# A state-space layer and a gated feed-forward block on one core: who copies the first turned quarter of tile 1, where tile 2 is turned, and the order of the fourth contraction step

## The chip, the cores and the metric

The kernel runs on one core of one Trainium2 chip. The metric is the time of one execution on the device in microseconds (us); the median of several runs is compared. Names used below: TensorE (PE) multiplies matrices and loads their stationary operands as separate instructions (PEld); VectorE (DVE), ScalarE (ACT) and GpSimd (POOL) work on elements; SyncE (SP) issues most DMAs. SBUF is the on-chip memory that all engines read; PSUM is the memory that TensorE writes, here eight banks of 128 partitions by 512 fp32 numbers.

## The reference

For `x` of 2048 tokens by 512 channels in bf16:

```
xn = layernorm(x)                                   # over the 512 channels
A  = state space: Bu = xn @ B_bar^T (complex, 512 states)
     h[t] = Lam_bar * h[t-1] + Bu[t];  2 * Re(h @ C^T) + xn * Dskip
B  = (gelu(xn @ w_gate) * (xn @ w_up)) @ w_down     # w_gate, w_up: 512 x 1376, w_down: 1376 x 512
out = x + A + B
```

The parts that this document is about are the first two products of B, `xn @ w_gate` and `xn @ w_up`, for the first 512 tokens.

## The kernel before

The tokens are worked in four blocks of 512, each block in four tiles of 128 tokens. For most of the kernel TensorE goes through `GU` (gate and up products, L843), `BU` (the input of the states, L749) and `DN` (the product with `w_down` and the states' output, L884), while VectorE runs the recurrence (L787).

The first block has to start before anything is normalised, while the weights are still arriving, and that start is what is changed here. Its tiles are not normalised first: a tile is only centred (the mean is subtracted, L961 for tiles 0 and 1, L950 for tiles 2 and 3), turned on TensorE (`cent_T`, L684, four transposes of 128 columns into one PSUM bank), and copied from PSUM into `XC` by ScalarE (L689). The division by the standard deviation comes later, as a scale of the gelu. The turned tile is the stationary operand of the gate and up products of its 128 tokens, so that the results have tokens on the partitions. The contraction over 512 channels has four steps `k`, each of which needs one quarter of the turned tile and one chunk of 128 rows of each weight; the chunks come as DMAs of 128 KB, gate and up in turn (L488).

For tiles 0, 1 and 2 and the first 512 of the 1376 columns the accumulation is spread out, one step at a time, so that a step can run as soon as its chunk has landed: `GT_k(k, j, u, ws)` (L701) is one matmul of step `k`, tile `j` and column half `u`, with `ws` telling whether it takes the gate weights (`[0]`, 256 columns), the up weights (`[1]`, 256 columns) or both side by side (`[0, 1]`, 512 columns). `ks(k, j, ws)` issues it for both halves. Six PSUM banks (`acc(j, u)`) hold the six running sums, gate in one half of the bank and up in the other; banks 6 and 7 take the transposes. After the fourth step `GT_evac` lets ScalarE take the gelu (L721) and VectorE multiply (L724). The ten groups that remain (tile 3, and columns 512 to 896 of all four tiles) run with all four steps at once in `GT_mm` (L712), tile 3 first:

```
        for (j, u), bank in zip([(3, 0), (3, 1), (0, 2), (0, 3), (1, 2), (1, 3), (2, 2), (2, 3), (3, 2), (3, 3)],
                                (6, 7, 0, 1, 2, 3, 4, 5, 0, 7)):
            GT_mm(j, u, bank)
            GT_evac(j, u, bank)
```

So the first `GT_mm` needs the whole of tile 3 in `XC`.

Order. TensorE and SyncE run their instructions in the order in which the source issues them. For VectorE, ScalarE and GpSimd a planner (`Sched`) sorts the instructions by costs written into the source; operations that are passed through `ch` stay in the order in which they were chained. A wait is a semaphore that the instruction itself, or a separate instruction just in front of it, waits for. An engine stands still at such a wait, and all that is queued behind it stands still too; only weight loads of TensorE are seen to run ahead of the matmul before them.

In front of the first groups TensorE runs seven matmuls on constants (L933). VectorE takes statistics with `stats` (L615, L616) and centres tile 2 after the statistics of tiles 0 and 2; those of tiles 1 and 3, the centring of tile 3, and the norms (L634) whose DMA transposes (`TR`, L736, on SyncE) feed the later `GU` of the same block come behind.

Of the kernel before, what the change touches and what calls it, by code (L numbers as in the profile page):

```python
# [9 lines left out]
ALU = mybir.AluOpType  # L10
# [336 lines left out]
L, D, P, F = 2048, 512, 512, 1376  # L347
# [7 lines left out]
def d_pe(n_list):  # L355
    return sum(n / 2.4 + 2.5 for n in n_list)
def d_dve_tt2x(n): return 100.0 + 0.52 * n
def d_dve_1x(n): return 100.0 + 1.04 * n
def d_dve_scan(n): return 90.0 + 2.08 * n
def d_dve_ts4x(n): return 220.0 + 0.26 * n  # L360
D_TINY = 160.0
def d_act(n, ptr=0): return 190.0 + 0.833 * n + 90.0 * ptr
# [3 lines left out]
def build(nc, ins, out):  # L366
    with ExitStack() as es:
# [6 lines left out]
        BANK = [Buf("bank%d" % i, "ps", i, i + 1) for i in range(8)]  # L374

        def ring(parent, name, n):
            return [A.sub(parent, "%s%d" % (name, i), i) for i in range(n)]
# [14 lines left out]
        X = ring(X_all, "X", NT)  # L392
        XN_all = A.alloc("XN", [8, D], BF16)
        XN = ring(XN_all, "XN", 8)
        DSKB = A.alloc("DSKB", [D], BF16)
        XD_all = A.alloc("XD", [NT, D], BF16); XD = ring(XD_all, "XD", NT)
        IDN = A.alloc("IDN", [128], BF16)
# [8 lines left out]
        MVt = [[A.sub(MV[b], "MV%d_%d" % (b, j), j) for j in range(4)] for b in range(NB)]  # L406
# [58 lines left out]
        V = lambda fn, dur, r, w, tag="", after=(): S.op("vector", fn, dur, r, w, tag, after)  # L465
        ACT = lambda fn, dur, r, w, tag="", after=(): S.op("scalar", fn, dur, r, w, tag, after)
        POOL = lambda fn, dur, r, w, tag="", after=(): S.op("gpsimd", fn, dur, r, w, tag, after)
        PE = lambda fn, dur, r, w, tag="": S.op("tensor", fn, dur, r, w, tag)
# [39 lines left out]
        def load_par():  # L508
            for q, nm in enumerate(("A_log_dt", "A_Lambda_re", "A_Lambda_im")):
                GATE["par"] = S.order_behind(S.dma(lambda e, q=q, nm=nm: e.dma_start(PROW.ap[4 * q:4 * q + 4, :], ins[nm].rearrange("(s p) -> s p", p=128)),  # L510
                      1024, writes=[PROWq[q]], tag="ld_" + nm, queue="scalar", after=[half]), GATE["par"])
            GATE["par"] = S.order_behind(ld_x0(2, "scalar"), GATE["par"])
# [100 lines left out]
        def stats(b, j):  # L613
            tt = 4 * b + j
            return (V(lambda e: e.bn_stats(ST[tt].ap, X[tt].ap), d_dve_1x(512), [X[tt]], [ST[tt]], "bnst"),  # L615
                    V(lambda e: e.bn_aggr(MVt[b][j].ap, ST[tt].ap), D_TINY, [ST[tt]], [MVt[b][j]], "bnag"))  # L616

        def root(b, j0, j1):
            mn, sbq, qb, rq = (cols(t, b, j0, j1) for t in (MN, SBQ, QB, RQ))
            mv = Buf("MV%d_%d_%d" % (b, j0, j1), "sb", MVt[b][j0].lo, MVt[b][j1 - 1].hi, MV[b].ap[:, j0:j1])  # L620
            op = V(lambda e: e.tensor_scalar(sbq.ap, mv.ap[:, :, 1], EPS_BF16, None, ALU.add), D_TINY, [mv], [sbq], "sbq")
            GATE["pow"] = POOL(lambda e: e.tensor_tensor(qb.ap, sbq.ap, HALF.ap[:, 0:j1 - j0], ALU.pow), 1100, [sbq, HALF], [qb], "pow")
            POOL(lambda e: e.tensor_copy(mn.ap, mv.ap[:, :, 0]), 200, [mv], [mn], "mn")
            return op, mn, qb, rq
# [48 lines left out]

        XCd = lambda j, k: XC_all.ap[:, k, 128 * j:128 * (j + 1)]

        XNp = [[Buf("XN%d_%d" % (j, n), "sb", XN[j].lo + 256 * n, XN[j].lo + (1024 if n else 256)) for n in range(2)] for j in range(2)]

        def cent_T(j, k0, k1, bank):
            pt = PS[bank].bitcast(BF16)[:, 0:128 * (k1 - k0)]

            def f(e):
                ins_ = None
                for k in range(k0, k1):
                    ins_ = e.transpose(pt[:, 128 * (k - k0):128 * (k - k0 + 1)], XN[j].ap[:, 128 * k:128 * (k + 1)], IDN.ap)  # L684
                return ins_
            PE(f, 56.0 * (k1 - k0), [XNp[j][k0 > 0] if j < 2 else XN[j], IDN], [BANK[bank]], "T0")
            dst, src = XC_all.ap[:, k0:k1, 128 * j:128 * (j + 1)], pt.rearrange("p (q t) -> p q t", t=128)
            w = XCs[j] if k1 - k0 == KD else [XCs[j][k0 > 0]]
            GATE["evTA"] = ACT(lambda e: e.activation(dst, src, ACTF.Copy), d_act(128 * (k1 - k0)), [BANK[bank]], w, "evT")  # L689

        FR = ((0, 256), (256, 512), (512, 768), (768, 896))

        def acc(j, u):
            return 2 * j + u

        def GT_k(k, j, u, ws, first=False):
            f0, f1 = FR[u]
            w = f1 - f0
            bank = acc(j, u)
            dst = PS[bank][:, w * ws[0]:w * (ws[-1] + 1)].rearrange("p (w f) -> p w f", w=len(ws))  # L700
            PE(lambda e: e.matmul(dst, XCd(j, k), WGU[:, ws[0]:ws[-1] + 1, k, f0:f1], start=first, stop=k == KD - 1, skip_group_check=True),  # L701
               d_pe([w * len(ws)]), [(WGc, WUc)[w_][k] for w_ in ws] + [XCs[j][k > 0]] + ([] if first else [BANK[bank]]), [BANK[bank]], "GK")
# [13 lines left out]
        def GT_evac(j, u, bank):  # L716
            f0, f1 = FR[u]
            w = f1 - f0
            GATE["nh"] = kk = (GATE["nh"] + 1) % 3
            sc, rb = rss[j]  # L720
            GATE["last_gelu"] = ACT(lambda e: e.activation(GG[kk].ap[:, 0:w], PS[bank][:, 0:w], ACTF.Gelu_apprx_tanh, scale=sc),  # L721
                                    d_act(w, 1), [BANK[bank], rb], [GG[kk]], "gelu")
            hp = Buf("H0_%d_%d" % (j, u), "sb", H0[j].lo + 2 * f0, H0[j].lo + 2 * f1)
            V(lambda e: e.scalar_tensor_tensor(H0[j].ap[:, f0:f1], PS[bank][:, w:2 * w], sc, GG[kk].ap[:, 0:w], ALU.mult, ALU.mult),  # L724
              d_dve_1x(w), [BANK[bank], GG[kk], rb], [hp], "hmul")
# [220 lines left out]
        def ch(*ops):  # L946
            for op in ops:
                tail_op[0] = S.order_behind(op, tail_op[0])
        def sub(j):
            return V(lambda e: e.tensor_scalar(XN[j].ap, X[j].ap, MVt[0][j].ap[:, 0:1], None, ALU.subtract),  # L950
                     d_dve_ts4x(512), [X[j], MVt[0][j]], [XN[j]], "sub")
        load_par()
        load_W()
        tr_par()
# [3 lines left out]
        def cent(j, n):  # L958
# [7 lines left out]
                                              op0=ALU.add, op1=ALU.add, accum_out=NM0.ap), 400, [X[0]], [H0[2], NM0], "mean0"))  # L966
        ch(cent(0, 0), cent(0, 1))
        cent_T(0, 0, 1, 7)
        ch(cent(1, 0), cent(1, 1))
        fill(1)  # L970
        cent_T(0, 1, 4, 5)
        def ks(k, j, w_, first=False):
            for u in range(2):
                GT_k(k, j, u, w_, first)
        cent_T(1, 0, 1, 6)
        ks(0, 0, [0], True)
        cent_T(1, 1, 4, 7)
        ks(0, 0, [1])
        ks(0, 1, [0], True)
# [2 lines left out]
        for w_ in range(2):  # L982
            for j in range(2):
                ks(1, j, [w_])
        ks(2, 0, [0]); ks(2, 1, [0]); ks(2, 0, [1])
        ch(*stats(0, 2)); ch(sub(2))
        cent_T(2, 0, 1, 6)
        cent_T(2, 1, 4, 7)
        ks(2, 1, [1])
        ks(0, 2, [0, 1], True)  # L990
        ch(*stats(0, 1))
        op, mn0, qb0, rq0 = root(0, 0, 3)
        ch(op)
        ch(*stats(0, 3)); ch(sub(3))
        ch(recip(qb0, rq0))
        op, mn3, qb3, rq3 = root(0, 3, 4)
# [5 lines left out]
        TR(0, [0, 1])  # L1002
        ks(1, 2, [0, 1])
        ks(2, 2, [0, 1])
        for j in range(3):
            GT_k(3, j, 0, [0, 1])
            if j == 0:
                cent_T(3, 0, 4, 6)
            GT_k(3, j, 1, [0, 1])
            for u in range(2):  # L1010
                GT_evac(j, u, acc(j, u))
        for (j, u), bank in zip([(3, 0), (3, 1), (0, 2), (0, 3), (1, 2), (1, 3), (2, 2), (2, 3), (3, 2), (3, 3)],
# [45 lines left out]
def bass_parallel_sum__ssm_conv_s5__geglu_ffn__prompt_kernel(  # L1058
    nc: bass.Bass,
    A_x: bass.AP,  # L1060
    A_Lambda_re: bass.AP,
    A_Lambda_im: bass.AP,
    A_B_re: bass.AP,
    A_B_im: bass.AP,
    A_C_re: bass.AP,
    A_C_im: bass.AP,
    A_log_dt: bass.AP,
    A_Dskip: bass.AP,
    B_x: bass.AP,
    B_w_gate: bass.AP,  # L1070
    B_w_up: bass.AP,
    B_w_down: bass.AP,
    out: bass.AP,
):
    ins = {
        "A_x": A_x, "A_Lambda_re": A_Lambda_re, "A_Lambda_im": A_Lambda_im,
        "A_B_re": A_B_re, "A_B_im": A_B_im, "A_C_re": A_C_re, "A_C_im": A_C_im,
        "A_log_dt": A_log_dt, "A_Dskip": A_Dskip,
        "B_w_gate": B_w_gate, "B_w_up": B_w_up, "B_w_down": B_w_down,
    }  # L1080
    build(nc, ins, out)
# [28 lines left out]
```

## Time and profile before

| | |
|---|---|
| median of 3 runs | 176.65 us (176.62 to 176.85) |
| profiled execution, its own time | 176.71 us |
| span in the profile, first to last instruction | 175.4 us |
| busy in the span: PE, DVE, ACT, POOL | 98%, 90%, 54%, 6% |
| granted TensorE clock | 1.00 |
| matmuls | 895, of which L701 36, L684 17 |
| first matmul on data; first `GT_mm`; last matmul (start) | 3.71, 10.79, 173.32 us |

A row of the timeline gives the start in us, the length in us (of several instructions in a row, from the first start to the last end), the engine, the line, the operation, what it writes and reads with sizes, how many, and in brackets the idle time of the engine in front of it and what ended that. The chain of waits gives start, length and what the chain that ended last consisted of. A table by stage gives the busy time of each engine in a stretch, with the number of instructions. A group of instructions by line and shape ends with its busy time in us, the mean ns of one, and the idle time in front of it. Matmuls are pipelined: the length of a row is longer than the distance from one start to the next, and it is the distance that costs time. Lines are those of the kernel before.

### The profile page before, as it was taken

Reading aid. Unit: us, or ns where it says so; the run is one execution under the profiler, and the core shown is the slowest. Engines: PE = TensorE matmul, PEld = TensorE weight load, DVE = VectorE, ACT = ScalarE, POOL = GpSimd, SP = SyncE. Lnnn points to the kernel's source line nnn. Section 1 sums busy time; section 2 is a strip of 40 time slices with the busy share of each in tenths; the row PEclk is TensorE's granted clock in tenths of the full one; section 3 lists DMA queues with packets and bytes.
Section 4 is the critical chain, followed back from the end, with each engine's and each line's share of the span. In section 5 each row is a group of like instructions: output and inputs, shape, how many; then the busy total and the mean of one; then the engine's idle time right before and its main releaser. Section 6 shows DMA issues by size and latency. Waiting matters only on the chain.

```text
span 175.4 us, 2533 instructions
## 1 busy us (share of the span) xinstructions
PE 172.7 (98%) x895; PEld 85.0 (48%) x895; DVE 158.5 (90%) x279; ACT 95.2 (54%) x187; POOL 9.9 (6%) x24
## 2 busy tenths in 40 slices
PE   8999999999999999999999999999999999999995
PEld 2646464845544444444644444444464444444454
DVE  5897999987989999789899999997999999999931
ACT  5476678999766997473676792000667970000000
POOL 4122220220000000002000000000000000000000
DMA  5999999477699400002024000002001000000312
GB/s 142 265 340 191 221 206 154 32 130 142 106 250 344 74 0 2 0 30 89 4 53 98 0 0 0 4 0 90 30 0 34 0 0 0 0 0 0 123 62 62
DMA packets 32421, 14.37 MB, mean 82 GB/s; under 512 B 23736, under 2 KB 32408, under 8 KB 32408
## 3 DMA queue, kind: packets, MB, share of 16 engines
q1 hardware_dynamic: 31952, 13.84, 34.6%
q10 hardware_dynamic: 456, 0.36, 0.6%
q8 instruction: 7, 0.11, 0.3%
q14 instruction: 6, 0.05, 0.1%
HBM read 6.46 MB, written 2.10 MB: 49 GB/s over the span
## 4 chain that ended last, share of the span: by engine, by line
PE 98%; DVE 0%; issue 0%
PE PS L884 37%; PE PS L843 32%; PE PS L749 16%; PE PS L712 4%; PE PS L701 3%; PE PS L817 3%; PE PS L933 2%; PE PS L684 1%; DVE arena L902 0%; PE PS L940 0%
## 5 line engine op out<-in xcount | busy, mean ns | idle before, releaser
L884 PE MATMUL PS<-arena 128*128 128x512 bf16 (+3 forms) x323 | 66.2, 366 | 0.0
L843 PE MATMUL PS<-arena 128*128 128x512 bf16 x264 | 58.1, 379 | 0.0
L884 PEld LDWEIGHTS PS<-arena 128*128 128x128 bf16 (+1 forms) x323 | 30.8, 98 | 35.2
L843 PEld LDWEIGHTS PS<-arena 128*128 128x128 bf16 x264 | 25.7, 98 | 30.3
L787 DVE TENSOR_TENSOR_SCAN arena<-arena 128x512 bf16<-128x512 f32 x32 | 38.8, 1252 | 0.0
L858 ACT ACTIVATE arena<-PS 128x512 bf16<-128x512 f32 x33 | 19.7, 598 | 27.0 <-PE PS L843 24.8
L749 PE MATMUL PS<-arena 128*128 128x512 bf16 (+1 forms) x144 | 28.2, 355 | 0.0
L862 ACT ACTIVATE arena<-PS 128x512 bf16<-128x512 f32 x33 | 19.7, 598 | 5.9 <-PE PS L843 5.8
L749 PEld LDWEIGHTS PS<-arena 128*128 128x128 bf16 x144 | 14.1, 98 | 13.3
L876 ACT ACTIVATE PS<-arena 128x512 f32<-128x512 bf16 (+2 forms) x17 | 9.4, 574 | 18.5 <-DVE arena L902 18.0
L758 ACT ACTIVATE arena<-PS 128x512 bf16<-128x512 f32 x32 | 17.4, 596 | 1.5 <-PE PS L749 1.5
L902 DVE TENSOR_TENSOR arena<-PS,arena 128x512 bf16<-128x512 f32 (+2 forms) x17 | 10.9, 652 | 7.8 <-PE PS L884 7.7
L864 DVE TENSOR_TENSOR arena<-arena 128x512 bf16<-128x512 bf16 x33 | 13.2, 413 | 1.8 <-ACT arena L862 1.6
L776 DVE TENSOR_TENSOR arena<-arena 128x4096 bf16<-128x4096 bf16 (+1 forms) x5 | 9.2, 1858 | 0.8 <-ACT arena L611 0.8
L774 DVE TENSOR_TENSOR arena<-arena 128x4096 bf16<-128x4096 bf16 (+1 forms) x5 | 9.2, 1853 | 0.0
L799 DVE TENSOR_TENSOR arena<-arena 128x4096 bf16<-128x4096 bf16 x4 | 9.1, 2286 | 0.0
L800 DVE TENSOR_TENSOR arena<-arena 128x4096 bf16<-128x4096 bf16 x4 | 9.1, 2284 | 0.0
L615 DVE BATCH_NORM_STATS2 arena<-arena 128x6 f32<-128x512 bf16 x12 | 7.8, 681 | 0.4 <-DMA arena<-in_A_x_dram 0.4
L721 ACT ACTIVATE arena<-PS,arena 128x256 bf16<-128x256 f32 (+1 forms) x16 | 6.3, 447 | 1.9 <-DVE arena L724 1.9
L712 PE MATMUL PS<-arena 128*128 128x512 bf16 (+1 forms) x40 | 7.1, 336 | 0.0
L724 DVE SCALAR_TENSOR_TENSOR arena<-PS,arena 128x256 bf16<-128x256 f32 (+1 forms) x16 | 6.2, 442 | 0.3 <-PE PS L701 0.3
L701 PE MATMUL PS<-arena 128*128 128x256 bf16 (+1 forms) x36 | 6.3, 309 | 0.0
(95 smaller groups left out, 123.4 us busy)
## 6 DMA issues: line engine op xcount, KB each, us to landing
out_dram<-arena SPq DMA_DIRECT2D x15, 128.0 KB, 1.7
arena<-in_A_x_dram SPq DMA_DIRECT2D x3, 512.0 KB, 5.3
arena<-in_B_w_down_dram SPq DMA_DIRECT2D x1, 1280.0 KB, 7.3
arena<-in_B_w_gate_dram SPq DMA_DIRECT2D x4, 128.0 KB, 3.3
arena<-in_B_w_up_dram SPq DMA_DIRECT2D x4, 128.0 KB, 3.2
arena<-in_B_w_gate_dram SPq DMA_DIRECT2D x1, 480.0 KB, 6.5
arena<-in_B_w_up_dram SPq DMA_DIRECT2D x1, 480.0 KB, 7.4
arena<-arena SPq DMA_TRANSPOSE x25, 3.1
```

Of the source, the lines that this page charges most:

```text
L701: PE(lambda e: e.matmul(dst, XCd(j, k), WGU[:, ws[0]:ws[-1] + 1, k, f0:f1], start=first, stop=k == KD - 1, skip_group_check=True), d_pe([w ...
L712: ins_ = e.matmul(dst, XCd(j, k), WGU[:, :, k, f0:f1], start=(k == 0), stop=(k == KD - 1))
L749: ins_ = e.matmul(PS[bank][:, 128 * j0:128 * j1], BBT[c][dk].ap[:, 128 * s:128 * (s + 1)], XNT[b].ap[:, dk, 128 * j0:128 * j1], start=(dk ...
L758: GATE["evBu"] = ACT(lambda e, bank=bank, k3=k3, s=s, c=c: e.activation(SSc[k3][s][c].ap, PS[bank][:, :], ACTF.Copy), d_act(512), [BANK[ba ...
L787: V(lambda e, g=g, rb=rb, init=init: e.tensor_tensor_scan(g.ap, rb, g.ap, init, ALU.mult, ALU.add), d_dve_scan(512), [g, PA[RRr]] + ([CARc ...
L843: ins_ = e.matmul(PS[bank][0:m, c0:c1], W.ap[:, dk, 128 * ft:128 * ft + m], XNT[b].ap[:, dk, c0:c1], start=(dk == 0), stop=(dk == KD - 1))
L858: GATE["last_gelu"] = ACT(lambda e, bg=bg, kk=kk, m=m: e.activation(GG[kk].ap[0:m, :], PS[bg][0:m, :], ACTF.Gelu_apprx_tanh), d_act(512), ...
L862: ACT(lambda e, bu=bu, kk=kk, m=m: e.activation(UPB[kk].ap[0:m, :], PS[bu][0:m, :], ACTF.Copy), d_act(512), [BANK[bu]], [UPB[kk]], "evU")
L864: V(lambda e, kk=kk, m=m, ft=ft, k2=k2: e.tensor_tensor(HTt[k2][ft].ap[0:m, :], GG[kk].ap[0:m, :], UPB[kk].ap[0:m, :], ALU.mult), d_dve_tt ...
L876: ACT(lambda e: e.activation(PS[bank][:, c0:c1], X[tt].ap[:, c0:c1], ACTF.Copy), d_act(c1 - c0), [X[tt]], [BANK[bank]], "seed")
L884: ins_ = e.matmul(PS[bank][:, c0:c1], l_[:, 128 * j:128 * (j + 1)], r_[:, c0:c1], start=False, stop=last and n == len(ops) - 1, skip_group ...
L902: V(lambda e: e.tensor_tensor(OUTB[ko].ap[:, c0:c1], PS[bank][:, c0:c1], XD[tt].ap[:, c0:c1], ALU.add), d_dve_1x(c1 - c0), [BANK[bank], XD ...
```

## The change

Three edits in the start of the first block.

1. The copy of tile 1's first turned quarter out of PSUM goes from ScalarE to VectorE (`vec=True`, chained behind the centring of tile 1 and in front of the statistics of tile 0). The two gate matmuls of step 0 for tile 0 are issued in front of tile 1's transposes, no more between the first and the other three.
2. Tile 2 is centred in two instructions, 128 columns and 384 columns, and the two up matmuls of step 2 for tile 1 go in between its first transpose and the other three, no more behind all four.
3. The fourth step (`k` = 3) of the three tiles is split. Gate and up ran as six matmuls of 512 columns, at the end. Now six gate matmuls of 256 columns are spread in front: two right after step 0 of tile 2, four after step 2 of tile 2; the six up matmuls of 256 columns follow at the end, with the transposes of tile 3 behind the first of them as they were behind the first matmul of 512 columns.

```
-        XNp = [[Buf("XN%d_%d" % (j, n), "sb", XN[j].lo + 256 * n, XN[j].lo + (1024 if n else 256)) for n in range(2)] for j in range(2)]
+        XNp = [[Buf("XN%d_%d" % (j, n), "sb", XN[j].lo + 256 * n, XN[j].lo + (1024 if n else 256)) for n in range(2)] for j in range(3)]
...
-        def cent_T(j, k0, k1, bank):
+        def cent_T(j, k0, k1, bank, vec=False):
...
-            PE(f, 56.0 * (k1 - k0), [XNp[j][k0 > 0] if j < 2 else XN[j], IDN], [BANK[bank]], "T0")
+            PE(f, 56.0 * (k1 - k0), [XNp[j][k0 > 0] if j < 3 else XN[j], IDN], [BANK[bank]], "T0")
...
+            if vec:
+                ch(V(lambda e: e.tensor_copy(dst, src), 200, [BANK[bank]], w, "evT"))
+                return
             GATE["evTA"] = ACT(lambda e: e.activation(dst, src, ACTF.Copy), d_act(128 * (k1 - k0)), [BANK[bank]], w, "evT")
...
-        def sub(j):
-            return V(lambda e: e.tensor_scalar(XN[j].ap, X[j].ap, MVt[0][j].ap[:, 0:1], None, ALU.subtract),
-                     d_dve_ts4x(512), [X[j], MVt[0][j]], [XN[j]], "sub")
+        def sub(j, n=None):
+            c0, c1 = (0, D) if n is None else ((0, 128), (128, D))[n]
+            return V(lambda e: e.tensor_scalar(XN[j].ap[:, c0:c1], X[j].ap[:, c0:c1], MVt[0][j].ap[:, 0:1], None, ALU.subtract),
+                     100 + 0.5 * (c1 - c0), [X[j], MVt[0][j]], [XN[j] if n is None else XNp[j][n]], "sub")
...
-        cent_T(1, 0, 1, 6)
         ks(0, 0, [0], True)
+        cent_T(1, 0, 1, 6, True)
         cent_T(1, 1, 4, 7)
         ks(0, 0, [1])
...
-        ch(*stats(0, 2)); ch(sub(2))
+        ch(*stats(0, 2)); ch(sub(2, 0)); ch(sub(2, 1))
         cent_T(2, 0, 1, 6)
+        ks(2, 1, [1])
         cent_T(2, 1, 4, 7)
-        ks(2, 1, [1])
         ks(0, 2, [0, 1], True)
+        ks(3, 0, [0])
         ch(*stats(0, 1))
...
         ks(1, 2, [0, 1])
         ks(2, 2, [0, 1])
+        ks(3, 1, [0])
+        ks(3, 2, [0])
         for j in range(3):
-            GT_k(3, j, 0, [0, 1])
+            GT_k(3, j, 0, [1])
             if j == 0:
                 cent_T(3, 0, 4, 6)
-            GT_k(3, j, 1, [0, 1])
+            GT_k(3, j, 1, [1])
             for u in range(2):
                 GT_evac(j, u, acc(j, u))
```

The planner is run anew and also sets some later VectorE instructions in another order (products of a later unit before or after a table's row, small coefficient operations, norms). The order on GpSimd and on SyncE is the same as before, that on ScalarE the same but for the copy that left it.

## The prediction

> **What bounds the kernel now.** The engines' shares come first: TensorE is busy 98% of the span. So I ask where it is not, in the chain of waits, which is TensorE's own queue nearly throughout:
>
> ```profile
> 4.68 0.22 PE PS L701 x2
> 4.90 0.17 PE PS L684 x3
> 5.07 2.27 PE PS L701 x20
> 7.34 0.22 PE PS L684 x4
> 7.56 1.67 PE PS L701 x8
> 9.23 0.04 issue
> 9.27 0.38 PE PS L701
> 9.65 0.22 PE PS L684 x4
> 9.87 1.08 PE PS L701 x5
> 10.95 6.93 PE PS L712 x40
> ```
>
> These pieces give the distances between starts without stalls. L701 x5 of 512 columns takes 1.08, so 0.216 us each; L684 x4 takes 0.22, so 0.055 per transpose; L712 has 24 of 512 and 16 of 256 columns, (6.93 - 24 x 0.216) / 16 = 0.109 per 256. Against these, L701 x20 should take 2.18, not 2.27; the x8 (two of 256, six of 512) 1.51, not 1.67; and one matmul costs 0.38 plus 0.04. From 10.8 us on the table by stage shows no idle time that could absorb anything:
>
> ```profile
> 10.80:17.70 6.90, 6.90 (x41) 3.90 (x40) 5.53 (x17) 5.11 (x14) 1.02 (x1) 1.00 1.02 255
> 17.70:173.60 155.90, 155.84 (x797) 75.90 (x795) 144.72 (x238) 84.97 (x162) 5.18 (x8) 1.00 0.30 64
> ```
>
> So whatever moves the first L712 moves the end by as much. The weight loads' timeline tells what the three stalls wait for:
>
> ```profile
> 5.20 0.23 PEld L701 LDWEIGHTS PS<-arena 128*128 128x128 bf16 x3 [0.19 <-ACT arena L689]
> 7.76 0.11 PEld L701 LDWEIGHTS PS<-arena 128*128 128x128 bf16 x2 [0.26 <-ACT arena L689]
> 9.24 0.10 PEld L701 LDWEIGHTS PS<-arena 128*128 128x128 bf16 x1 [0.50 <-issue]
> ```
>
> The first two end with a ScalarE copy (of tile 1's and of tile 2's first quarter). Matmuls start at 5.20 where 4.91 + 2 x 0.109 = 5.12 was due (stall 0.08) and at 7.76 where 7.40 + 2 x 0.109 = 7.62 was due (0.15). The third, marked "issue", is the weights' arrival: the last up chunk is issued at 4.99 and lands 4.1 later, at 9.1 (DMA issues by line); its matmul starts at 9.27, 0.20 later than 8.85 + 0.216 = 9.07. ScalarE's timeline has the copies:
>
> ```profile
> 4.06 0.28 ACT L689 ACTIVATE arena<-PS 128x128 bf16<-128x128 bf16 x1
> 4.49 1.11 ACT L689 ACTIVATE arena<-PS 128x384 bf16<-128x384 bf16 x3
> 7.43 0.66 ACT L689 ACTIVATE arena<-PS 128x128 bf16<-128x128 bf16 x2 [1.84 <-PE PS L684]
> 9.91 0.60 ACT L689 ACTIVATE arena<-PS 128x512 bf16<-128x512 bf16 x1 [1.82 <-PE PS L684]
> ```
>
> **Edit 3, the fourth step.** Gate chunk 4 is issued at 4.52 and lands 3.6 later, at 8.1; the first gate matmul of step 4 comes at 7.76 + 2 x 0.216 = 8.19, just about in time. The up chunk is now needed only after 0.65 us more of matmuls, so the 0.20 stall goes. Twelve matmuls of 256 in place of six of 512 cost 12 x 0.109 - 6 x 0.216 = 0.01. [...]
>
> What is late next is tile 3's copy. The first L712 needs all of tile 3: from the first transpose to the last result 0.38 (row of L684 at 9.49, x4), 0.04 to ScalarE (9.87 to 9.91), 0.60 for the copy, 0.05 to the next weight load (as from 7.71, the end of tile 2's first copy, to 7.76): 1.07 in all. Before, 4 x 0.055 + 5 x 0.216 = 1.30 of TensorE's own work lay over it, with 0.23 to spare. Now only five matmuls of 256 are behind the transposes: 0.22 + 0.55 = 0.77. New stall: 0.30.
>
> Position of the transposes: 9.49 + 7 x 0.109 - 0.216 - 0.20 = 9.84; plus 1.07 gives the first L712 at 10.91, against 10.79: **+0.12**, plus whatever the front loses (d). What hides a lateness in the front before, the weights' arrival, is gone: d now counts in full.
>
> **Edit 2.** From tile 2's first transpose (7.18) to step 0 of tile 2 the copy's chain takes 7.76 - 7.18 = 0.58. TensorE's work between them was four transposes and two matmuls and stays that; it only changes places. So the 0.15 stall stays. The other three transposes come 0.22 later: start 7.46, results 0.33 later, 0.04, copy 0.49, 0.05: 8.37. Step 1 of tile 2 now comes at 8.19 + 0.22 = 8.41: hidden by 0.04, and worth a few hundredths if not. The second centring instruction costs VectorE 0.14 (0.40 from the first of the L961 pair to the L615 behind it, against 0.26 from L950 to L615).
>
> **Edit 1.** VectorE's rows near it:
>
> ```profile
> 4.50 0.69 DVE L615 BATCH_NORM_STATS2 arena<-arena 128x6 f32<-128x512 bf16 x1
> 5.80 0.69 DVE L615 BATCH_NORM_STATS2 arena<-arena 128x6 f32<-128x512 bf16 x1 [0.40 <-DMA arena<-in_A_x_dram]
> ```
>
> and by shape, its operations on 128 columns of PSUM:
>
> ```profile
> L724 DVE SCALAR_TENSOR_TENSOR arena<-PS,arena 128x128 bf16<-128x128 f32 x4 | 1.4, 344 | 0.0
> ...
> L902 DVE TENSOR_TENSOR arena<-PS,arena 128x128 bf16<-128x128 f32 x1 | 0.3, 291 | 0.4 <-PE PS L884 0.4
> ```
>
> Step 0's gate pair now stands in front of tile 1's first transpose, and it waits for the copy of tile 0's first quarter, which ends at 4.34. One wait costs 0.05, a second in front of the same load about 0.10 (the up chunk's landing, 9.14 at most, to 9.24): the pair starts between 4.39 and, as before, 4.51; I take 4.47. Plus 0.23 (4.51 to 4.74 before): tile 1's first transpose at 4.70, not 4.41; result 0.22 later, 0.04 to the copy: VectorE starts at 4.96. No row shows its copy of bf16 from PSUM. Bounds: 0.165 (the 16-element cast L564) and 0.344 (L724 at 128); nearest are 0.291 (L902 at 128, from PSUM) and 0.255 (L961 at 128, from SBUF): I take 0.27. Plus 0.05: tile 1's step 0 at 5.28, against 5.20. **d = +0.08**. ScalarE loses a copy of 0.28, and its next one, of tile 1's other three quarters, has to wait for their transposes anyway. [...]
>
> Bounds of d: cheap ends (4.39, cast) would bring it to -0.10, but then step 4's gate matmuls arrive before their chunk, and d is held at about -0.02. Dear ends (4.51, a first transpose of 0.27 as at 4.41, copy 0.344) give +0.25.
>
> Queued behind the copy on VectorE are the statistics of tile 0, 0.6 later than 4.50. The idle 0.40 in front of 5.80 takes up most of it; some 0.2 is left, so tile 2's first centring (128 columns, 0.255) ends at 7.2, and TensorE, at 7.18 + d, meets it nearly in step: no term. Behind, tile 3's centring ends at 9.3 + 0.3, its transposes start at 9.9: covered. Norms come 0.3 later and so do the four transposing DMAs that SyncE issues from 9.95 to 15.13; first read at 17.71. The smallest later cover that I find is 0.6 (L724 ends 17.09, L843 starts 17.71), and VectorE's new order puts that product earlier.
>
> **Sum.** -0.20 (up chunk) + 0.01 + 0.30 (tile 3's copy) + 0.08 = +0.20 with roundings. The profiled execution took 176.71 (its span 175.37 and 1.34 around it), 0.06 above the median: 176.91 against it, **176.85** against the median 176.65. That is 0.11%, inside the 0.2% (0.35 us) that a measurement of this kernel can tell from no change.
>
> **Rivals.** *Slower:* VectorE's copy is the dear one, so that tile 1's step 0 is the new front. If its start takes the 0.11 that VectorE needed behind a gelu (10.87 to 10.98) in place of 0.04, with the other dear ends, that step starts at 5.52, d = 0.32, total +0.44: 177.09. It decides from 5.43 on (d over 0.23). For it: no row has this copy, every unknown in front of it adds, and nothing behind absorbs it. Against: the nearest rows.
> *Faster:* the three stalls go as the edits address them, and tile 3's copy hides: -0.08 - 0.15 - 0.20 + 0.01 = -0.42, 176.23. For it: the stalls are the only ones after 5 us. Against: 1.07 needed against 0.77 given. It decides if the first L712 starts before 10.4. That the planner undoes the order is excluded: TensorE runs in source order.
>
> **How the numbers follow.** Forecast 0.54, dear front 0.37, stalls gone 0.09. The forecast lies within 0.2% but for 0.03 at its upper end: slower 0.40, same 0.51, faster 0.09. Range: from d = -0.02 (+0.10) less 0.07 for the runs' spread, 176.68, to the dear front and a little above, 177.16; the faster case and a little of the dear one stay out. The forecast alone: 176.70 to 177.02.
>
> **What would show it.** Right: no wait on a DMA near 9.2; a weight load of L712 (L715 in the new numbering) that waits some 0.3 for ScalarE's copy of 512; first group near 10.99; the stall in front of tile 2's step 0 still 0.15; a PSUM copy on VectorE of 0.25 to 0.29 from about 4.96. Wrong: no wait in front of the first group, a wait of over 0.1 for the gate chunk, or any idle TensorE after 11 us.

## The result, and the profile after

The changed kernel is slower: 177.40 us median of 8 runs (177.22 to 177.87), against 176.86 for the kernel before beside it, ratio 1.0032 (95% interval 1.0020 to 1.0044). Two later comparisons of the same two kernels gave 1.0019 (1.0006 to 1.0032) and 1.0017 (1.0001 to 1.0032). At 177 us these are +0.57, +0.34 and +0.30 us, where the prediction said +0.20. The kernel before moved too: its median was 176.65 in the three runs of the start, and 176.86, 177.02, 177.09, 177.09 and 177.01 in the comparisons that followed.

The profiled execution of the changed kernel took 177.46 us, its span is 176.1. I look first at whether the loss lies in front of the first `GT_mm` (now L715) or behind it, with the table by stage; the columns are as before the change.

```profile
11.50:17.90 6.40, 6.38 (x36) 3.54 (x37) 5.86 (x18) 5.47 (x14) 1.02 (x1) 1.00 1.02 189
17.90:174.30 156.40, 155.59 (x786) 76.37 (x799) 144.85 (x236) 85.25 (x162) 5.17 (x8) 1.00 0.31 65
```

TensorE is busy throughout; the 0.8 us that the second row lacks are missing records (886 matmuls are recorded here, 901 in other profiles of kernels with edit 3). From the first `GT_mm` to the last matmul it takes 162.54 us (11.52 to 174.06), and took 162.53 before (10.79 to 173.32). So in this pair of executions all of the difference is in front: 11.52 against 10.79. The chain of waits of that stretch has two pieces that are not TensorE's:

```profile
3.57 3.94 DMA arena<-in_B_w_up_dram
7.51 0.04 issue
7.55 0.39 PE PS L704 x2
...
10.61 0.24 PE PS L684 x4
10.84 0.02 issue
10.87 0.61 ACT arena L692
11.47 0.05 issue
11.52 0.61 PE PS L715 x2
```

The weight loads' timeline gives the four places where TensorE stood still after 5 us. These are the rows of it in front of which the idle time, in brackets, ends on another engine or a DMA:

```profile
5.33 1.86 PEld L704 LDWEIGHTS PS<-arena 128*128 128x128 bf16 x18 [0.29 <-DMA arena<-in_B_w_up_dram]
7.55 0.11 PEld L704 LDWEIGHTS PS<-arena 128*128 128x128 bf16 x2 [0.36 <-DMA arena<-in_B_w_up_dram]
...
8.37 1.95 PEld L704 LDWEIGHTS PS<-arena 128*128 128x128 bf16 x13 [0.16 <-ACT arena L692]
...
11.51 0.55 PEld L715 LDWEIGHTS PS<-arena 128*128 128x128 bf16 x4 [0.42 <-ACT arena L692]
```

Measured by the distances between matmul starts, the stalls are 0.29 (up chunk 1, landed 5.29), 0.24 (up chunk 3, landed 7.51), 0.15 (tile 2's first copy) and 0.31 (tile 3's copy). The last up chunk landed at 8.59, and nothing waits for it. Tile 3's copy and VectorE's copy are these rows, from the timelines of ScalarE and of VectorE:

```profile
10.87 0.60 ACT L692 ACTIVATE arena<-PS 128x512 bf16<-128x512 bf16 x1 [1.95 <-PE PS L684]
```

```profile
5.08 0.23 DVE L690 COPY arena<-PS 128x128 bf16<-128x128 bf16 x1 [0.48 <-PE PS L684]
```

The two waits for weights are new, but nothing in the change touches those DMAs. Whether the change causes them, or this execution merely had them, one pair of profiles cannot say. That is what the experiments are about.

### The profile page after: what moved, and what is told of

The parts are those of the page before. It is cut to its first block, busy times and chain, and to the rows that moved or that the text cites. A ratio compares the mean times of both kernels' runs of the same rounds, so it can differ in the third digit from the quotient of the medians.

```text
span 176.1 us, 2527 instructions
## 1 busy us (share of the span) xinstructions
PE 172.3 (98%) x886; PEld 85.9 (49%) x901; DVE 159.3 (90%) x281; ACT 95.6 (54%) x186; POOL 10.0 (6%) x24
## 4 chain that ended last, share of the span: by engine, by line
PE 94%; DMA 2%; SPq 1%; issue 1%; ACT 0%; DVE 0%
PE PS L887 37%; PE PS L846 32%; PE PS L752 16%; PE PS L715 4%; PE PS L820 3%; DMA arena<-in_B_w_up_dram 2%; PE PS L704 2%; SPq L488 1%; ACT arena L692 0%; PE PS L684 0%; SPq L497 0%; DVE arena L905 0%
## 5 line engine op out<-in xcount | busy, mean ns | idle before, releaser
L846 PE MATMUL PS<-arena 128*128 128x512 bf16 x257 | 57.1, 379 | 0.4
L846 PEld LDWEIGHTS PS<-arena 128*128 128x128 bf16 x264 | 25.8, 98 | 30.2
L715 PE MATMUL PS<-arena 128*128 128x512 bf16 (+1 forms) x40 | 7.1, 337 | 0.1
```

The source lines that it names most:

```text
L715: ins_ = e.matmul(dst, XCd(j, k), WGU[:, :, k, f0:f1], start=(k == 0), stop=(k == KD - 1))
L846: ins_ = e.matmul(PS[bank][0:m, c0:c1], W.ap[:, dk, 128 * ft:128 * ft + m], XNT[b].ap[:, dk, c0:c1], start=(dk == 0), stop=(dk == KD - 1))
```

## The experiments

Three theories. **L**: landings differ from execution to execution; tile 3's copy costs its 0.30 always, and the credit for the last up chunk exists only in executions that have that wait. **F**: what the prediction missed is the front, edit 1. **D**: the change makes the chunks land later. A ratio stands for the time against the kernel before, on the same chip, with its 95% interval; a stall is the distance between two matmul starts less what that distance is without a stall (0.055, 0.109, 0.216 us by columns).

### Each edit alone

Edit 1 alone:

```
-        cent_T(1, 0, 1, 6)
         ks(0, 0, [0], True)
+        cent_T(1, 0, 1, 6, True)
```

> Only edit 1 (VectorE copies tile 1's first turned quarter, step 0's gate pair in front of tile 1's transposes). Theory L (landings: the loss is tile 3's copy, 0.30, plus a front later by 0.1 to 0.2, and the up chunk's arrival near 9.1 gives back up to 0.20 in those executions only in which it is late): +0.0 to +0.2 us against the kernel before, tile 1's step 0 at 5.3 or later, and a late up chunk absorbs part. Rival F (the whole unforeseen 0.35 us is the front, whatever the weights do): +0.35 to +0.45 us.

Measured: 177.30 against 177.02, 1.0013 (1.0002 to 1.0025), so +0.23 us. That lies between L's range and F's, and the interval (+0.04 to +0.44) reaches into both, so it decides nothing between them. VectorE's copy takes 0.22 again. In its profile no weight chunk is waited for; instead matmuls of 256 columns start 0.213 apart, not 0.109, until 6.6 us.

Edit 2 alone (tile 2 centred by `sub(2, 0)` and `sub(2, 1)`, and the order):

```
         cent_T(2, 0, 1, 6)
+        ks(2, 1, [1])
         cent_T(2, 1, 4, 7)
-        ks(2, 1, [1])
```

> Only edit 2 (tile 2 centred and turned in two parts, the up pair between). Theory L: 0.0 to +0.05 us, the stall in front of tile 2's step 0 stays at about 0.15. Rival F: the same. If the edit worked as its place suggests, -0.15 us.

Measured: 177.11, 1.0004 (0.9996 to 1.0013). Without the gate pair of step 4 in between, the copy of the other three quarters is late too; and this execution does have the wait for the last up chunk (landed 9.37). Weight loads:

```profile
7.80 0.11 PEld L701 LDWEIGHTS PS<-arena 128*128 128x128 bf16 x2 [0.15 <-ACT arena L689]
8.40 0.55 PEld L701 LDWEIGHTS PS<-arena 128*128 128x128 bf16 x4 [0.48 <-ACT arena L689]
9.48 0.10 PEld L701 LDWEIGHTS PS<-arena 128*128 128x128 bf16 x1 [0.54 <-issue]
```

By starts: 0.15, 0.16 and 0.24.

Edit 3 alone:

```
         ks(0, 2, [0, 1], True)
+        ks(3, 0, [0])
...
         ks(2, 2, [0, 1])
+        ks(3, 1, [0])
+        ks(3, 2, [0])
         for j in range(3):
-            GT_k(3, j, 0, [0, 1])
+            GT_k(3, j, 0, [1])
...
-            GT_k(3, j, 1, [0, 1])
+            GT_k(3, j, 1, [1])
```

> Only edit 3 (fourth step as gate of three tiles, then up). A wait of about 0.30 us in front of the first L712 group in every theory. Theory L: +0.12 us in executions in which the up chunk is late for the kernel before, up to +0.32 us in those in which it is early; about +0.2 to +0.3 in the median. Rival F: at most +0.12 us, since the rest is edit 1's.

Measured: 177.70, 1.0031 (1.0018 to 1.0044). This is more than any theory said, for a reason of its own: the planner now puts the first gelu in front of tile 3's copy on ScalarE (first fence), and the small coefficient operation L558, which waits for GpSimd, in front of products on VectorE (second fence).

```profile
10.45 0.47 ACT L721 ACTIVATE arena<-PS,arena 128x256 bf16<-128x256 f32 x1 [2.01 <-PE PS L701]
10.82 0.59 ACT L689 ACTIVATE arena<-PS 128x512 bf16<-128x512 bf16 x1
```

```profile
16.50 0.16 DVE L558 TENSOR_TENSOR arena<-arena 128x4 f32<-128x4 bf16 x1 [2.50 <-POOL arena L557]
16.60 1.27 DVE L724 SCALAR_TENSOR_TENSOR arena<-PS,arena 128x256 bf16<-128x256 f32 x3
```

The first group waits 0.51, not 0.31, and TensorE stands 0.53 at 17.6 us for the products queued behind L558. So this run does not price edit 3 as it sits in the changed kernel. The next version does: one line holds the gelu behind the copy.

```
+            if (j, u) == (0, 0):
+                S.order_behind(GATE["last_gelu"], GATE["evTA"])
```

> Edit 3 alone, as in a3_gateup_alone, but with the first gelu of the three tiles held behind tile 3's copy on ScalarE. Both theories: the first group waits 0.31 for tile 3's copy, not 0.51, and the 0.5 us stall near 17.6 is gone. Theory L (weights land when they like; tile 3's copy counts in full, the up chunk's late landing is given back only in executions that have it): +0.20 to +0.35 us against the kernel before. Theory F (the unforeseen part is the front, that is edit 1): +0.12 us or less.

Measured: 177.33 against 177.09, 1.0012 (0.9998 to 1.0026), +0.21 us. The wait is 0.31 again and the stall at 17.6 is gone. Inside L's range; F's bound of 0.12 lies inside the interval too. Its profile has one wait that the three of the changed kernel do not have, 0.31 in front of the first gate matmul of step 4:

```profile
8.52 1.52 PEld L701 LDWEIGHTS PS<-arena 128*128 128x128 bf16 x11 [0.64 <-DMA arena<-in_B_w_gate_dram]
```

Gate chunk 4 landed at 8.48 here, and at 7.62 to 8.35 in the other 17 profiles. By taking gate first, edit 3 needs this chunk near 8.2: it gives up a wait for the last up chunk and takes on one for gate chunk 4, where that is late.

Edits 2 and 3 without edit 1, the gelu held as above:

> Edits 2 and 3 without edit 1 (ScalarE copies tile 1's first quarter as before, the step-0 pair behind its transpose), the first gelu held behind tile 3's copy. Theory L: +0.25 to +0.40 us against the kernel before. Theory F: +0.15 us or less, since the front is that of before.

Measured: 177.28, 1.0012 (0.9998 to 1.0027). Close to edit 3 alone, and between L's range and F's bound of 0.15. In its profile the waits are those of the changed kernel, 0.15 and 0.31, and no chunk is waited for; it took 177.81 because the half rate lasted to 6.6 us (d3_before_fourth, with the half rate as long and without tile 3's wait, took 177.45). Against the 1.0019 that the whole change had in the same call, leaving edit 1 out gave 0.12 us, less than these intervals can tell.

### Is it the order or the engine in edit 1?

The changed kernel with one line moved, and the gelu held as above:

```
-        ks(0, 0, [0], True)
         cent_T(1, 0, 1, 6, True)
+        ks(0, 0, [0], True)
         cent_T(1, 1, 4, 7)
```

> The changed kernel with VectorE's copy kept, but the two gate matmuls of step 0 back behind tile 1's first transpose as before the change; the first gelu held behind tile 3's copy. It tells the order of issue from the choice of the engine. If the order is what edit 1 costs: 0.10 to 0.20 us less than the changed kernel, VectorE's copy near 4.7, tile 1's step 0 near 5.0 to 5.2. If VectorE's copy itself is what costs: no gain against the changed kernel.

Measured: 177.25, 1.0011 (0.9997 to 1.0025), beside 1.0019 of the changed kernel in the same call: 0.14 us less, with an interval that holds zero. VectorE's copy starts at 4.75 and no weight load waits for it, so the choice of the engine costs nothing that this trace shows; the order may.

### Without tile 3's wait

The changed kernel, with tile 3's transposes three matmuls of 256 columns earlier:

```
         ks(3, 1, [0])
+        cent_T(3, 0, 4, 6)
         ks(3, 2, [0])
...
-            if j == 0:
-                cent_T(3, 0, 4, 6)
```

> The changed kernel with one thing moved: tile 3's transposes stand two matmul pairs earlier, in front of the gate pair of tile 2's fourth step, so that eight matmuls of 256 columns and not five lie over the copy. Every theory: the wait in front of the first full group (0.31 us in the changed kernel's profile) goes below 0.05 us, so 0.27 to 0.31 us less than the changed kernel. Against the kernel before, theory L: +0.1 to +0.3 us; rival F: +0.25 us or more.

Measured: 177.18, 1.0005 (0.9994 to 1.0015), +0.09 us, just under L's range and well under F's 0.25, with an interval (-0.11 to +0.27) that reaches both. The same on edit 3 alone:

> Edit 3 alone with tile 3's transposes earlier (as in a4). Theory L: no wait for the up chunk and none in front of the first full group; 0.0 to -0.2 us against the kernel before, according to how late the up chunk is in the median. Rival F: -0.1 to -0.2 us.

Measured: 177.04, 0.9997 (0.9980 to 1.0013), inside L's range. In both the first group's weight load waits for nothing; these are the rows of the first and of the second:

```profile
11.15 0.77 PEld L715 LDWEIGHTS PS<-arena 128*128 128x128 bf16 x5
```

```profile
11.10 0.99 PEld L712 LDWEIGHTS PS<-arena 128*128 128x128 bf16 x6
```

This is the clearest split of the study. Eight comparisons of kernels whose first group waits for tile 3's copy gave 1.0011 to 1.0032, mean 1.0019; seven in which it does not gave 0.9991 to 1.0013, mean 1.0002. The difference, 0.0017 of 177 us, is 0.30 us, about the wait's own length. The kernels of the two groups differ in other things too: without a3_gateup_alone, which has losses of its own, it is 0.27, and without d1_t3_and_x2_early (below), which covers one more wait, 0.23.

### Without the weights' landings

Here every accumulating matmul of tiles 0 to 2 reads gate chunk 1, so that none can wait for another chunk (those columns of the output are then not the reference's). Once on the kernel before, once on the changed one:

```
-            PE(lambda e: e.matmul(dst, XCd(j, k), WGU[:, ws[0]:ws[-1] + 1, k, f0:f1], ...
+            mov = WG.ap[:, 0, 0:w * len(ws)].rearrange("p (w f) -> p w f", w=len(ws))
+            PE(lambda e: e.matmul(dst, XCd(j, k), mov, ...
```

> The kernel before, but every accumulating matmul of the first three tiles reads the first gate chunk alone (so gate and up of these columns are not what the reference has, and no matmul of them waits for chunks 2 to 8). Theory L: the stalls on weights go, those on the two copies (0.08 and 0.15) stay; 0.1 to 0.4 us less than the kernel before, by as much as its executions lose to landings. Rival D (the change itself makes the chunks land later): the same.

> The changed kernel with the same substitution. Against the kernel before with the substitution (b1): theory L +0.40 to +0.48 us (tile 3's copy 0.30, twelve matmuls for six 0.01, front 0.1 to 0.16); rival F +0.65 us or more; rival D (the change makes the chunks land later, and that is the unforeseen part) +0.20 to +0.40, that is, clearly less than the 0.54 us of the full kernels.

Measured: 1.0000 (0.9985 to 1.0015) and 1.0016 (1.0003 to 1.0029), medians 176.96 and 177.41. The difference of the two is 0.28 us. L had expected the first 0.1 to 0.4 under the kernel before and the difference at 0.40 to 0.48; both missed, and 0.28 lies in the range that D had, 0.20 to 0.40. But the pair is less clean than it was meant to be. In b1_before_one_chunk TensorE, no longer held up by chunks, waits for VectorE's centring of tile 2 (0.41) and of tile 3 (0.10) instead; x tile 2 landed at 6.16 there, at 5.78 in the first profile of before:

```profile
7.54 0.23 PEld L684 LDWEIGHTS PS<-arena 128*128 128x128 bf16 x4 [0.53 <-DVE arena L951]
...
9.76 0.23 PEld L684 LDWEIGHTS PS<-arena 128*128 128x128 bf16 x4 [0.43 <-DVE arena L951]
```

In b2_after_one_chunk the first group waits 0.40 for tile 3's copy, not 0.31: it is now the first to read the later chunks, and its weight load starts 0.11 after the copy's end (0.04 in the changed kernel). So taking every wait for a chunk out of the kernel before, the 0.20 for the last up chunk included, gained nothing that can be measured, at least in part because other waits stand right behind. And with no chunk to wait for, the change still costs about what the two later comparisons of the whole kernels give, 0.34 and 0.30, which leaves little for D; the landings themselves, in the next section, say more.

### More profiles of the same two kernels

> The kernel before once more, for a second profile of it: how the landings of the eight weight chunks differ from one execution to the next. Theory L: chunks land at times that differ by 0.3 us or more from the first profile, in either direction, and the stalls with them; the sum of the stalls goes with the execution's own time. Rival D: landings as in the first profile.

> The kernel before, unchanged, for one more profile: does TensorE wait for up chunk 4 in front of 9.3 us, as in the first profile of it (0.20), or not, as in the second? Theory L: in some executions 0.1 to 0.2, in others none. If the wait belongs to every execution that starts as early as the first: 0.15 to 0.25.

> The same as d2_before_third, for a fourth profile of the kernel before. Theory L: landing of up chunk 4 anywhere from 8.1 to 9.4 us, wait 0 to 0.25.

> The changed kernel once more, for a second profile of it beside the others of this call. Theory L: +0.45 to +0.60 us again; the wait for tile 3's copy is 0.30 again, while the waits for weight chunks in front of it and the end of the half-rate stretch lie elsewhere. Theory D (the change itself makes the chunks land later): the up chunks land as late as in the first profile of it, 5.3 and 7.5 us.

> The changed kernel, unchanged, for a third profile and a third comparison. Theory L: the wait for tile 3's copy is 0.30 to 0.31 again and the time 0.3 to 0.55 us above the kernel before. Theory F: the front (first transpose to tile 1's step 0) is later than in the kernel before by 0.3 us or more in each of the profiles.

The kernel before against itself gave 1.0005 (0.9994 to 1.0016) in b3_before_again, the two repeats of the changed kernel the ratios told above: +0.34, under L's 0.45 to 0.60, and +0.30, the low end of its 0.3 to 0.55. Times in us; "full rate" is when matmul starts go from twice the distance to the distance of the prediction, "late" is the wait of the first `GU` matmul behind the groups (L843, now L846). The first profile of after has the two waits for up chunks 1 and 3, 0.53 together, that are told above; no other of the seven has one for those chunks.

| profile | its own time | full rate from | last up chunk lands | wait for it | wait for tile 3 | first group | late |
|---|---|---|---|---|---|---|---|
| before, first | 176.71 | 4.5 | 9.14 | 0.20 | 0 | 10.79 | 0 |
| b3_before_again | 177.00 | 5.8 | 8.26 | 0 | 0 | 11.09 | 0 |
| d2_before_third | 177.22 | 6.2 | 8.72 | 0 | 0 | 11.26 | 0 |
| d3_before_fourth | 177.45 | 6.6 | 8.39 | 0 | 0 | 11.49 | 0 |
| after, first | 177.46 | 4.8 | 8.59 | 0 | 0.31 | 11.52 | 0 |
| c2_after_again | 177.21 | 4.5 | 8.61 | 0 | 0.31 | 10.98 | 0.27 |
| d4_after_third | 177.48 | 5.1 | 8.46 | 0 | 0.31 | 11.19 | 0.37 |

Against D: in c2_after_again and d4_after_third up chunk 1 landed at 4.96 and 4.79 and up chunk 3 at 6.84 and 7.13, where D expected 5.3 and 7.5 again, and nothing waits for them; in the four profiles of before they landed at 4.03 to 4.95 and at 6.42 to 6.99. The last up chunk landed no later after the change than before. So the two waits for weights of the first profile of after belong to that execution. Small shifts of the landings cannot be excluded by three profiles.

The wait for the last up chunk is in one of four profiles of the kernel before. In the other three the chunk lands 0.4 to 0.9 earlier, and TensorE arrives later, because its matmuls ran at half their rate for longer. None of the three shows an execution as early as the first, but at their landings, 8.26 to 8.72, it would not have waited either: its matmul was due at 9.07. The chain of waits of the third profile shows that; the same pieces of the first profile, in the prediction, took 0.22, 0.17 and 2.27:

```profile
4.64 0.43 PE PS L701 x2
5.07 0.32 PE PS L684 x3
5.39 2.62 PE PS L701 x20
8.01 0.22 PE PS L684 x4
8.23 1.89 PE PS L701 x9
10.12 0.22 PE PS L684 x4
10.35 1.08 PE PS L701 x5
```

Two matmuls of 256 columns take 0.43 instead of 0.22. No wait stands beside them, and the granted clock of the table by stage, the third number from the right, reads 1.00 in both stretches (fourth profile, where the rate is half up to 6.6):

```profile
4.00:6.50 2.50, 2.50 (x17) 1.79 (x16) 1.68 (x5) 1.48 (x5) 0.00 (x0) 1.00 0.96 311
6.50:8.00 1.50, 1.50 (x16) 1.32 (x15) 1.42 (x4) 0.00 (x0) 0.00 (x0) 1.00 0.88 223
```

The trace's own record of the clock is silent in front of that change: in the second, third and fourth profile of before it begins, at full clock, at 5.76, 6.16 and 6.50, just where the distances change. That the clock was lower until then is my reading; no record shows it. The table shows 1.00 for a stretch that has no record, too: the first profile of before has no record at all, and 1.00 in every row.

The last column of my table is a wait that the prediction had priced at nothing. In c2_after_again and d4_after_third the first `GU` matmul waits for the last of the four transposing DMAs (a weight load that waits for "issue", as with the up chunk):

```profile
10.97 0.98 PEld L715 LDWEIGHTS PS<-arena 128*128 128x128 bf16 x6 [0.42 <-ACT arena L692]
```

```profile
18.16 0.99 PEld L846 LDWEIGHTS PS<-arena 128*128 128x128 bf16 x6 [0.36 <-issue]
```

```profile
11.19 0.76 PEld L715 LDWEIGHTS PS<-arena 128*128 128x128 bf16 x5 [0.42 <-ACT arena L692]
```

```profile
18.47 0.77 PEld L846 LDWEIGHTS PS<-arena 128*128 128x128 bf16 x5 [0.45 <-issue]
```

(The first two are of c2_after_again, the other two of d4_after_third.) That DMA landed at 18.05 and 18.36; in the four profiles of before and the first of after it landed at 16.29 to 16.95, though it was issued at 13.76 to 14.24 in all of them. Just in these two of the seven a fetch of instructions runs among the transposes (DMA queues from 14 to 19 us, number of packets, MB and share; first c2_after_again, then d4_after_third):

```profile
q8 instruction: 1, 0.02, 1.4%
```

```profile
q8 instruction: 1, 0.02, 1.8%
```

The packet starts at 15.5. In the other five its first packet of 16 KB comes at 20.1 to 21.9. Of all 18 profiles of this study four have it at 15.5 (these two, a4_after_t3_early and c1_gateup_gelu_behind), these four alone have the fourth DMA landing at 18.0 or later, and in them the first `GU` matmul waits 0.27, 0.37, 0.06 and 0.09. That the fetch delays the DMA is so far a coincidence of four in four, not a test. All four are of kernels with edit 3; of the other seven profiles of such kernels none has it, and none of the seven profiles without edit 3. Whether the change brings it about stays open.

### A version without both waits

Edit 3 with the early tile 3; x tile 2 loaded in front of the three parameter rows on ScalarE's queue, and tile 2's transposes in front of four, not two, matmuls:

```
         def load_par():
+            GATE["par"] = S.order_behind(ld_x0(2, "scalar"), GATE["par"])
...
-        ks(2, 0, [0]); ks(2, 1, [0]); ks(2, 0, [1])
+        ks(2, 0, [0]); ks(2, 1, [0])
...
         cent_T(2, 1, 4, 7)
+        ks(2, 0, [1])
         ks(2, 1, [1])
```

> A version that might beat both: the order of b4_gateup_t3_early (edit 3 with tile 3's transposes in front of the last two gate matmuls of the fourth step), and the two up matmuls of step 2 for tile 0 behind tile 2's transposes, which x tile 2 is loaded for in front of the three parameter rows on ScalarE's queue. If tile 2's copy is then covered: no 0.15 stall in front of tile 2's step 0, no stall in front of the first group, 0.10 to 0.25 us less than the kernel before wherever no chunk is late. If the landings set the pace (theory L), some of it is taken back by a wait for a chunk of the third or fourth step: 0 to -0.15 us. If the earlier load of x tile 2 delays the first weight chunks: a stall before 5.5 us and no gain.

Measured: 176.77 against 177.01, 0.9991 (0.9975 to 1.0007). x tile 2 lands at 5.07 (5.59 to 6.06 in the kernel before), and its profile has a single wait after 5 us, for an up chunk:

```profile
5.35 2.33 PEld L701 LDWEIGHTS PS<-arena 128*128 128x128 bf16 x18 [0.17 <-DMA arena<-in_B_w_up_dram]
7.70 0.32 PEld L684 LDWEIGHTS PS<-arena 128*128 128x128 bf16 x4
7.97 2.10 PEld L701 LDWEIGHTS PS<-arena 128*128 128x128 bf16 x14
```

The 0.15 in front of tile 2's step 0 is covered, as is tile 3's copy. Its median is 0.24 us under that of before beside it (0.16 by the ratio), the most of all versions; the interval of the ratio still holds 1, so a gain is not shown. No second comparison of this version was measured, nor the early x tile 2 without the rest.

## Why the prediction was wrong

**Tile 3's copy, +0.30: right.** The wait is 0.31 in each of the three profiles, and taking it away brings the changed kernel back to 0.09 us above the kernel before (-0.11 to +0.27). The twelve matmuls in place of six start 0.109 apart, as the 0.01 of the sum had it.

**Edit 2: right.** The stall in front of tile 2's step 0 is 0.15 in all three, and the other three quarters are hidden behind the gate pair (without it, 0.16 in a2_tile2_alone).

**The front, d = +0.08: right where the execution was like the one it was worked out on.** c2_after_again is such an execution: full rate from 4.5, as in the first profile of before. There tile 1's first transpose starts at 4.73 (predicted 4.70), its step 0 at 5.27 (5.28), the first group at 10.98 (10.99). VectorE's copy took 0.22 to 0.23, less than the 0.27 assumed; the dear front was not what happened. That 5.27 meets 5.28 is luck in part: the gate pair started at 4.51, not 4.47, and the cheaper copy made up for it. In the first profile of after the gate pair still ran slowly (0.166 and 0.177 for 0.109), so the transpose came at 4.83 and the copy at 5.08. Edit 1 alone measured +0.23, and leaving it out or turning its order back gave 0.12 and 0.14 less: F may have something in it, of 0.1 to 0.2 us, that no interval here separates from the 0.08. As the whole cause it is out: F expected a front later by 0.3 or more in every profile of after, and in c2_after_again tile 1's step 0 is 0.07 later than in the first profile of before.

**The up chunk, -0.20: the step that failed, for the median.** As arithmetic it held: c2_after_again against the first profile of before is 10.98 - 10.79 = +0.19, with that credit in it. But the credit belongs to one profile of the kernel before in four (a2_tile2_alone, with the old order of the fourth step, has the wait too; of all 18 profiles the chunk lands after 9.0 in four). Where the chunk is not late the same sum is 0.01 + 0.30 + 0.08 = +0.39. The three comparisons, +0.57, +0.34 and +0.30, lie around this sum; the +0.20 with the credit is outside the interval of the first (+0.35 to +0.78) and inside those of the other two. The page of before had the hint: the median from issue to landing of the up chunks was 3.2 us, this one took 4.15; with 3.2 it lands at 8.2, 0.9 ahead of its matmul. A stall that hangs on one DMA being slow in one execution is no property of the kernel, and its removal should have been taken at 0 with -0.20 as an end of the range.

**"The smallest later cover that I find is 0.6": failed as well.** The last DMA behind the norms does not land at the same time in every execution: its cover was 1.3 in the first profile of before (landed 16.40, read from 17.71) and gone in two of three profiles of after, which lose 0.27 and 0.37 there. In the pair c2_after_again and first profile of before, +0.19 in front and +0.27 here make up +0.46 of the +0.50 between their own times. How often this happens, with and without the change, three and four profiles cannot tell; so the shares of the two failures in the median stay open.

**The base.** The median 176.65 came from three runs; the same kernel's later medians were 0.21 to 0.44 higher. The profile shown was near that low end: of the four it has the earliest full rate. Of the 0.55 between 177.40 and 176.85, 0.21 is the base (176.86 for 176.65) and 0.34 the change (0.54 for 0.20).

## What to carry to other kernels

A stall that ends with a DMA's landing must be held against the usual landing of its like before its removal is credited; a stall that ends with an engine's own chain (tile 3's copy, 1.07 needed, 0.77 covered) was there in every profile of the changed kernel and could be priced to 0.01 us from one profile. Where several things in a start-up absorb each other, what lies behind all of them counts in full (here tile 3's wait of 0.31), and what is won in front can be taken up by the next wait, as in b1_before_one_chunk (0.41 and 0.10). And when matmuls are moved ahead to fill a wait, look at what they were covering: here the gate halves, moved in front of tile 3's transposes, uncovered the copy behind these, and moving the transposes forward too took most of the loss back.

## What the runs showed of the hardware

Matmul starts were twice as far apart in the first microseconds (0.107 and 0.213 at 128 and 256 columns), and the change to 0.055 and 0.109 came anywhere from 4.5 to 6.6 us in profiles of the same two kernels, 3.7 to 5.8 us after the first matmul at 0.77, worth up to 0.7 us at the first group (10.79 to 11.49 in the four profiles of before). In eight of the 18 profiles the trace has a record of the clock; its first entry, at 5.23 to 6.65, falls where the distances change. What sets the moment no run shows.

A single 16 KB fetch of instructions at 15.5 us went with the last transposing DMA landing 1.1 to 2.1 us later in c2_after_again and d4_after_third (18.05 and 18.36) than in the other five profiles of the two kernels (16.29 to 16.95); in the four profiles that have such a fetch there, 0.06 to 0.37 us of TensorE's time went with it.
